# A finer, re-ordered job schedule with paired remainders and eight named PSUM banks in an attention-plus-MLP kernel

## The chip, the cores and the metric

The kernel runs on one core of one Trainium2 chip. The core has TensorE (PE, matmuls; the loading of its weights is shown apart as PEld), VectorE (DVE), ScalarE (ACT), GpSimd (POOL), and SyncE (SP), which here only issues DMAs. Matmul results land in PSUM, which has eight banks of 128 x 512 float32. POOL can't read PSUM, so every bank is emptied by ACT or DVE. The metric is device microseconds for one execution, taken as the median of a few runs; lower is better.

## What is computed

One sequence of 2048 tokens with 512 features. `xn` is the layer norm of `x`. The output is `x` plus attention over `xn` plus an MLP over the layer norm of `xn`:

```python
def _A_ref(x, wq, wk, wv, wo, beta):          # 32 heads of 16, 4 segments of 512 tokens
    for s in range(N):
        qs, ks, vs = q[:, :, s], k[:, :, s], v[:, :, s]
        logits = einsum("bhqd,bhkd->bhqk", qs, ks) * scale + mask
        p = softmax(logits);  a_dot = einsum("bhqk,bhkd->bhqd", p, vs)
        pq = phi(qs);  num = einsum("bhld,bhde->bhle", pq, M);  den = einsum("bhld,bhd->bhl", pq, z) + 1e-6
        o = g * num / den + (1.0 - g) * a_dot
        pk = phi(ks);  M = M + einsum("bhld,bhle->bhde", pk, vs);  z = z + sum(pk)
    return o @ wo
def _B_ref(x, w1, b1, w2, b2):                # 512 -> 1792 -> 512
    return gelu(layernorm(x) @ w1 + b1) @ w2 + b2
xn = layernorm(x)
return x + _A_ref(xn, ...) + _B_ref(xn, ...)
```

The mask is causal within a segment; `phi(t)` is `t + 1` where `t > 0` and `exp(t)` elsewhere.

## The kernel before

**Units.** Attention is cut into 16 units: 4 segments times 4 groups of 8 heads. The MLP is cut into 16 pieces `j`: 8 blocks of 256 tokens times two halves of the 1792 hidden features. Most operands are float32 values split into a high and a low float16, so a product is three matmuls.

**Jobs.** All work is a list of small jobs. `streams()` gives lists of jobs that keep their own order, `ORDER` is one long string in which each letter names a stream, and `plan()` walks the string, takes the next job of the named stream and calls its function. The kernel has a manual schedule: each engine gets its instructions in the order in which the jobs issue them, and waits on semaphores where it needs another's result. So the string is the schedule, for PE and for the queues of ACT, DVE, POOL and SP alike.

The jobs that matter, with their letters as used below:

- `T` (`qk_proj`, matmuls on line 459): projects the queries or keys of a unit, 12 matmuls of 512 columns; ACT and DVE make the high and low halves (477, 481), SP sends them to DRAM, ACT and DVE form `phi` (480, 486 to 492). `Tr` reads them back in a layout in which two heads lie on partitions 0 to 49 and 64 to 113.
- `M` (`m_jobs`, 584 and 591): products of queries with keys, two heads at a time, each in one half of PE's rows and each into its own bank; DVE adds the mask and takes the row maximum. A unit has 12 such jobs: for each of four head pairs one with query block 3 (512 columns), one with blocks 2 and 0 (384 + 128), one with block 1 (256 columns, so half of each bank is used). `R` (`m_row`, 599) turns the maxima into rows, which go over DRAM (`md`) into the query operand (`Rr`).
- `S` (`s_jobs`, 626 and 631): scores transposed, keys on partitions, again two heads in two halves of PE and two banks; ACT takes the exponential into `pt`, POOL zeroes what the causal mask forbids (640). 12 jobs a unit: key block 0 (512 columns), blocks 1 and 3 (384 + 128), block 2 (256).
- `pv`, `PV` (655): the value product, four heads at a time in four column strips of PE; `O` (`o_norm`, 679 to 691): the division and the split of the result; `out` (777): the output projection, added to the token's row `acc` and stored (`st`).
- `K`, `N`, `Z`, `Qd`, `Q`: the memory state `M`, `z` and its use (505 to 568).
- `D` (459 with `w1s`): one hidden tile of the MLP, 12 matmuls of 256 columns; `G` (723): gelu over a piece, with a table load on each side (723 and 839); `H` (730 to 732): split of the activation in POOL, ACT, POOL; `e`, `E` (759): second product, three matmuls of 512 columns, summed over seven jobs in one bank, then added to `acc` by DVE (763).
- `X`, `Y`, `Xt`, `Yt`: layer norm and transposes (385 to 448). `wl`, `wm`, `wf`, `ws`: load of the weights, sums of squares (299), scale (332 to 350), split into two float16 (362 to 367). `hold` (273): a memset of one column that makes the weight loads behind it wait.

**PSUM.** Seven banks are a rotating pool `dense`, and the eighth, `eacc`, is kept for the sum of the MLP's second product.

**SP.** One queue holds nearly all DMAs in the order of the jobs; only the bias rows (740) go out on POOL's queue.

Of the kernel before, what the change touches and what calls it, by code (L numbers as in the profile page):

```python
# [19 lines left out]
P = 128  # L20
D = 512
# [33 lines left out]
NAMES = "abcdefghijklmnopqrstuvwxyzABCDEFGHIJKLMNOPQRSTUVWXYZ"  # L55


def streams():
    keys, queries, nat, qk_back, maxi, m_back, soft, vals_p, heads, memo, vals, norm, again, hid, act, mlp, outs, accs, wts = (
        [] for _ in range(19))  # L60
    for i in range(NU):
        s, g = divmod(i, NG)
        keys.append(("T", i, 1))
        queries.append(("T", i, 0))
        qk_back += [("Tr", i, 1), ("Tr", i, 0)]
        m_back.append(("Rr", i))
        maxi += [("M", i, n) for n in range(12)] + [("R", i)]
        for h, ts in enumerate(((0, 2), (1, 3))):
            soft += [("S", i, t, n) for t in ts for n in range(3)]
            vals_p += [("pv", i, h, kb) for kb in range(3)] + [("PV", i, h)]  # L70
        heads += [("O", i, k) for k in range(3)]
        if s:
            memo += [("Z", i), ("Qd", i), ("Q", i)]
        if s < NSEG - 1:
            nat.append(("N", i))
            memo.append(("K", i))
        if g == 0:
            vals += [("V", s, b) for b in range(4)]
            outs += [("out", s, b) for b in range(4)]
    norm += [("X", 0, 0, 0), ("X", 0, 1, 0), ("X", 0, 0, 1), ("X", 0, 0, 2), ("X", 0, 1, 2)]  # L80
    for n in range(NSEG):
        for b in range(2):
            norm += [("X", n, b, k) for k in range(3)] * (n > 0) + [("Xt", n, b, k) for k in range(2)]
    for n in range(2 * NSEG):
        again += [("Y", n, 0, 0), ("Y", n, 0, 2), ("Yt", n, 0, 0), ("Yt", n, 0, 1)]
    for j in range(NU):
        hf, fh = divmod(j, 2)
        hid += [("D", j, f) for f in range(FH)]
        act += [("G", j)] + [("H", j, c) for c in range(4)]
        for a in range(2):  # L90
            if fh == 0:
                accs += [("A", 2 * hf + a, k) for k in range(2)]
            mlp += [("e", j, a, f) for f in range(FH - 1)] + [("E", hf, a, fh)]
    for m in PARTS:
        wts += [("wl", m, k) for k in range(LOADS[m])]
        if m == "qk":
            wts.append(("hold",))
        if m == "v":
            wts.append(("par",))
    split = [[("wm", m, k) for k in range(SQUARES[m])] + [("wf", m)] + [("ws", m, c) for c in range(len(SPLIT[m]))] +  # L100
             [("gate",)] * (m == "v") for m in PARTS]
    zero = [("zero", 0), ("const",), ("zero", 1)]
    return [norm, again, wts, [("par2",)], zero, keys, queries, nat, qk_back, maxi, m_back, soft, vals_p, heads, memo, vals,
            hid, act, mlp, outs, accs, [("st", n) for n in range(4 * NSEG)]] + split
# [3 lines left out]
    "aacawweeacccccwccaccwawxxxaaxbxxaceyyxxxxdfcbzzzcycxxAizbyyxzgbzyiczAzhzqqAzqqyzqBABjjjAucqgAqjujrpjrjBAcjBAjf"  # L108
    "srpsjjsjAsrbAipsujByikCrcCpssoBjsCsBCjBlBqBssljlquljqljBlsqjjDmBmmmjqhjblsjllsqlljqojlCbrCmmcmmjbakCfCqCqriqnq"
    "rginllhqsallsnugllqojjjmmDmCCmqsCljslljlrrujjjjflssljsarjjmiumimmsDsrssjasrnhsrskDnqasssjlqnjllsaaqlllsqqjjmmm"  # L110
    "umarjqjlslsjlaqljsasljsbljsDjjDbfsmmmmrbjssrnokbDgDssqrqinollqqllilqqljsnsjrjjmmmmqjrlsjlsshljlsjlsqjlsjjjmmmm"
    "rofpjinropnkgnipllsltvulltvlujjprjjjmmmmosjljsjltvblujjslblotvjjlsmrmmmsjhnskrnssfsqloqsilulqlollsgqinqqmmmmbo"
    "llossjlsljusljshsljbjmmmuramrjqunjqrnfqjqrsijjsoqnjjsrsssoqjskgsqqslallsssaslilsolrrjqjjjummjmmharjssjlqjarssl"
    "jlasjljrsljqsjlaqksmsmammnoqnssaqslsalblsbofnllioolbgbmmmmbhiqllqqllqjlqjlqjromrmmmjnjrnfppjjsjopjjjspsjorsojn"
    "rksbightvslllitvllsqljsosjjjmmmmjtvljsuusuljlusslljtljjsvrmrmmmnjjqrnqqqjkfssroqrsiqllsnollsgillsquosbmmmmbssl"
    "osjllsjslsjlsljhrujarjmmmmjnjqrnqfuisqsjssrjjorjqqssonjksgssoasslllsssllqqilrajjqrjjqqjarmmmmjjsarljssrssjljsl"
    "salllaqjsasusmmmmnqjqnqhjskassoanbsofllblolillgbimmmmobollflqljlqljqjjrmmmmrnjjrqqpnbjjjsrspsjjosspjoqnjkigtvr"
    "sslllpoliltvljssbjjjmmmmqjlsljssljlssljtvjrjtvjrlmmjqusjmrmnsrnkfqssllsqouqurqqulolliluusgoqsnmmmmibsllsbsslls"
    "sjljqjlursjmmmmqrnjrjnfjqqrssjisjjoqssrjjqoqsjsrkgssisrsnqrqllolssqsqljrlsjrjsssjlsjmmjjmmqljqljslljljjqlsjkru"
    "mmmmssnrnsslllssslllnossmmmmrllllsllorsrmmmmnsssssnnssssstvtvtvtv"  # L120
# [3 lines left out]
def plan():  # L124

    todo = [iter(st) for st in streams()]
    tab = "E"
    for c in "".join(ORDER):
        key = next(todo[NAMES.index(c)])
        k = key[0]  # L130
        need = "G" if k == "G" else "E" if k in ("S", "Qd") or k == "O" and key[2] == 0 or k == "T" and (
            key[1] >= NG if key[2] == 0 else key[1] < NU - NG) else tab
        yield key, None if need == tab else need
        tab = need
# [3 lines left out]
def infini_mixer_kernel(ctx: ExitStack, tc: tile.TileContext, x, wq, wk, wv, wo, beta, w1, b1, w2, b2, out):  # L138
# [216 lines left out]
    def w_split(m, n):  # L355
# [5 lines left out]
        if SPLIT[m][n] == "V":  # L361
            A.activation(h, r, AF.Copy, scale=s)
            V.scalar_tensor_tensor(l, r, s, h, op0=OP.mult, op1=OP.subtract)
        else:
            G.tensor_scalar(r, r, s, 0.0, op0=OP.mult, op1=OP.add)
            A.activation(h, r, AF.Copy)
# [39 lines left out]
    def norm_apply(tok, tiles, twice, act):  # L406
        for j, t in enumerate(tiles):
# [8 lines left out]
    def ln(kind, n, b, part):  # L416
# [11 lines left out]
        else:  # L428
            norm_apply(tok, lt[kind, n, b], kind == "Y", (kind, n, b) == ("X", 0, 1))
# [38 lines left out]

    def qk_proj(i, which):
        s, g = divmod(i, NG)  # L470
        w, rows, d = ((wqs, (0, 32, 16), qd[i % 2]), (wks, (0, 16, 32), kd[i % 2]))[which]
# [5 lines left out]
        A.activation(hl[:, 0, :], p, AF.Copy, scale=float(2 ** -16))  # L477
        if phi:
            e = sb.tile([P, 512], F32, name=("phq", "phk")[which])
            A.activation(e, p, AF.Exp, scale=qkcol(2, 1 - which, g))  # L480
        V.scalar_tensor_tensor(hl[:, 1, :], p, float(2 ** -16), hl[:, 0, :], op0=OP.mult, op1=OP.subtract)  # L481
# [3 lines left out]
        if phi:  # L485
            V.tensor_scalar(e, e, 1.0, qkcol(3, 1 - which, g), op0=OP.min, op1=OP.mult)
            if which == 0:
                V.scalar_tensor_tensor(e, p, 0.0, e, op0=OP.max, op1=OP.add)
            else:
                if s:  # L490
# [378 lines left out]
```

## Time and profile before

| what | value |
|---|---|
| median of 3 runs | 762.66 us (762.06 to 762.82) |
| span of the profiled execution | 761.0 us |
| TensorE busy | 723.0 us, 95% of the span, 5189 matmul records |
| VectorE busy | 547.7 us, 72% |
| ScalarE busy | 528.8 us, 69% |
| GpSimd busy | 353.7 us, 46% |
| mean granted TensorE clock | 0.989 of full speed |

The span runs from the first to the last instruction of one profiled execution; the median of the runs stands 1.66 us above it. Durations below come from this execution. Times in a row of the timeline are the start and then the length, both in us; matmuls overlap, so the distance from one start to the next tells more than the length. A float32 matmul has two records on PE in some cases, so 5189 records are 4595 matmuls of the program. A granted clock below 1 means that PE ran a part of the stretch at half speed. "Idle before" and "<-" tell how long an engine stood still ahead of a row and what it had waited for.

### The profile page before, as it was taken

To read this page: it belongs to the slowest core of one execution; us is meant where nothing else is said; L and a number is where in the kernel's file an instruction comes from. 1 tells how busy PE (TensorE), PEld (TensorE's weight loads), DVE (VectorE), ACT (ScalarE), POOL (GpSimd) and SP (SyncE) were. 2 spreads that over 40 slices of the span, in tenths; PEclk is the share of its full clock that TensorE was granted. 3 is DMA by queue.
4 is the path that set the end of the run, shared out by engine and by line. 5 is a ranking of instruction groups with operands and counts; after the bars stand their busy time and mean duration, and the time that the engine had idled before them with its cause. 6 is when DMAs were issued, how large, how long until landed. Compare 5 with 4: busy or idle time off the path is not lost.

```text
span 761.0 us, 14513 instructions
## 1 busy us (share of the span) xinstructions
PE 723.0 (95%) x5189; PEld 378.0 (50%) x5189; DVE 547.7 (72%) x1677; ACT 528.8 (69%) x908; POOL 353.7 (46%) x544
## 2 busy tenths in 40 slices
PE   2689999999999999999999999999999999999987
PEld 1364565455644455554454455455555445455433
DVE  5599878898685857888567674979759574777622
ACT  5887898778785568485783577758585577856970
POOL 4465646654524443453434163536335235345461
PEclk9899999999999999999999999999999999999989
DMA  6975213411203224120311324131240314211001
GB/s 184 328 202 157 74 47 103 92 43 52 63 22 112 78 71 100 44 69 19 102 39 39 101 66 118 36 79 30 52 124 1 93 43 104 64 45 43 17 1 56
DMA packets 54085, 59.16 MB, mean 78 GB/s; under 512 B 5039, under 2 KB 40893, under 8 KB 54013
## 3 DMA queue, kind: packets, MB, share of 16 engines
q1 hardware_dynamic: 51708, 54.04, 24.8%
q0 software_dynamic: 2304, 4.20, 3.4%
q8 instruction: 41, 0.67, 0.4%
q14 instruction: 32, 0.25, 0.1%
HBM read 41.18 MB, written 17.04 MB: 77 GB/s over the span
## 4 chain that ended last, share of the span: by engine, by line
PE 83%; ACT 7%; DVE 5%; issue 2%; DMA 1%; POOL 1%; SPq 1%; DVEq 0%; ACTq 0%; POOLq 0%
PE dense L459 33%; PE eacc L759 18%; PE dense L655 9%; PE dense L777 6%; PE dense L626 5%; PE dense L584 5%; ACT pt L631 2%; PE dense L532 2%; PE dense L540 1%; PE dense L560 1%; PE dense L444 1%; DMA mhl<-in_B_b_dram 1%; DVE dense L591 1%; ACT hT L723 1%; DMA nN<-in_A_x_dram 1%
## 5 line engine op out<-in xcount | busy, mean ns | idle before, releaser
L591 DVE CUSTOM_DVE_ANT_0 dense<-dense,mask 128x512 f32<-128x512 f32 (+3 forms) x512 | 241.3, 516 | 21.5 <-PE dense L584 14.0
L631 ACT ACTIVATE pt<-dense,qkcs 128x512 f32<-128x512 f32 (+1 forms) x384 | 205.5, 627 | 31.5 <-PE dense L626 31.2
L759 PE MATMUL eacc<-w2s,hT 128*128 128x512 f16 x672 | 171.6, 382 | 2.0 <-DVE acc L763 1.0
L640 POOL TENSOR_SCALAR_AFFINE_SELECT pt<-pt 128x256 f32<-128x256 f32 x256 | 101.0, 424 | 141.9 <-ACT pt L631 141.2
L459 PE MATMUL dense<-yT,w1s 128*128 128x256 f16 x1344 | 161.4, 273 | 2.9 <-DVE yT L448 2.1
L459 PEld LDWEIGHTS <-w1s 128*128 128x128 f16 x1344 | 127.8, 98 | 36.9 <-issue 15.2
L732 POOL TENSOR_TENSOR hT<-hh,hT 128x512 f16<-128x512 f32 x64 | 69.2, 1081 | 88.2 <-ACT hT L731 88.2
L759 PEld LDWEIGHTS <-hT 128*128 128x128 f16 x672 | 58.6, 98 | 78.2 <-issue 26.4
L655 PE MATMUL dense<-pt,vt 128*32 128x512 f32 (+3 forms) x1024 | 79.0, 440 | 0.1
L591 DVE DVE_READ_ACCUMULATOR2_ANT mc<- 128x1 f32 x512 | 72.6, 142 | 0.0
L731 ACT ACTIVATE hT<-hh 128x512 f16<-128x512 f32 x64 | 36.6, 572 | 42.8 <-POOL hh L730 42.7
L584 PE MATMUL dense<-kst,qst 48*128 48x512 f16 (+3 forms) x512 | 62.8, 300 | 1.8 <-ACT pt L631 0.9
L626 PE MATMUL dense<-qst,kst 50*128 50x512 f16 (+3 forms) x512 | 61.2, 301 | 2.5 <-ACT pt L631 1.4
L730 POOL TENSOR_SCALAR hh<-hT,sc 128x512 f32<-128x512 f32 x64 | 42.6, 666 | 40.6 <-ACT hT L723 38.4
L481 DVE SCALAR_TENSOR_TENSOR hl<-dense,hl 128x512 f16<-128x512 f32 x32 | 22.0, 688 | 54.7 <-ACT phq L480 40.1
L655 PEld LDWEIGHTS dense<-pt,vt 128*32 128x32 f32 x1024 | 32.6, 110 | 45.7 <-issue 32.3
L716 ACT ACTIVATE hT<-dense,b1t,sc 128x256 f32<-128x256 f32 x64 | 36.0, 564 | 18.9 <-PE dense L459 18.3
L459 PE MATMUL dense<-xnT,wks 128*128 128x512 f16 x192 | 48.2, 405 | 0.0
L459 PE MATMUL dense<-xnT,wqs 128*128 128x512 f16 x192 | 45.8, 390 | 0.1
L459 PE MATMUL dense<-wvs,xnT 128*128 128x512 f16 x192 | 43.9, 379 | 0.1
L777 PE MATMUL dense<-wos,oT 128*128 128x512 f16 x192 | 43.7, 380 | 0.0
L626 PEld LDWEIGHTS <-kst 50*128 50x128 f16 x512 | 21.2, 94 | 43.5 <-issue 36.8
(223 smaller groups left out, 951.5 us busy)
## 6 DMA issues: line engine op xcount, KB each, us to landing
xt<-in_A_x_dram SPq DMA_DIRECT2D x30, 256.0 KB
kd<-hl SPq DMA_DIRECT2D x48, 128.0 KB
kst<-kd SPq DMA_DIRECT2D x32, 192.0 KB
qd<-hl SPq DMA_DIRECT2D x48, 128.0 KB
qst<-qd SPq DMA_DIRECT2D x32, 192.0 KB
acc<-in_A_x_dram SPq DMA_DIRECT2D x16, 256.0 KB
acc<-in_B_b_dram POOLq DMA_DIRECT2D x16, 256.0 KB, 4.3
out_dram<-acc SPq DMA_DIRECT2D x16, 256.0 KB
```

Source lines behind the costliest of these rows:

```text
L459: T.matmul(p, wsl(ws, k, a), xsl(xs, k, b), start=s0 and i == 0, stop=s1 and i == 3 * n - 1)
L584: T.matmul(p[:, o:o + n], stk[i, 0][r, t, P * qb:P * qb + P], stk[i, 1][r, t, :n], start=True, stop=True)
L591: V.tensor_tensor_reduce(p[:, o:o + n], p[:, o:o + n], mask[:, 512 - n:], 1.0, -3e38, OP.add, OP.max, mc[i][:, 4 * b + t, qb:qb + 1])
L626: T.matmul(p[:, o:o + n], stk[i, 1][r, t, P * kb:P * kb + P], stk[i, 0][r, t, P * kb:], start=True, stop=True)
L631: A.activation(e[:, OFF[kbs[0]]:OFF[kbs[0]] + o], p[:, :o], AF.Exp, scale=qkcs[:, 1, i % NG:i % NG + 1])
L640: G.affine_select(v, v, pattern=[[0, 2], [1, P]], compare_op=OP.is_ge, fill=0.0, base=0, channel_multiplier=-1)
L655: T.matmul(p[32 * c:32 * c + 32, P * kb:], vt[s, kb][:, 4 * g + c, 16 * odd:16 * odd + 32], pt[i, 2 * c + odd][:, OFF[kb]:OFF[kb] + LEN[kb ...
L730: G.tensor_scalar(t, hz[:, z, :], col(SHH + j % 2), 0.0, op0=OP.mult, op1=OP.add)
L731: A.activation(hT[:, z, 0, :], t, AF.Copy)
L732: G.tensor_tensor(hT[:, z, 1, :], t, hT[:, z, 0, :], op=OP.subtract)
L759: T.matmul(p, t[:, u, P * a:P * a + P], w2s[:, fo, v, :], start=fi == 0 and n == 0, stop=fi == FH - 1 and n == 2)
L777: T.matmul(p, o[:, u, P * b:P * b + P], wos[:, g, v, :], start=i == 0, stop=i == 3 * NG - 1)
```

## The change

- **Finer jobs.** Several jobs are cut in two to six, each with its own stream, so that the string can place the parts apart: `T` into projection, low half with its DMAs (`Tv`) and `phi` (`Tw`); `S` into scores and the causal selects (`Sg`); `O` into six steps; `H` and `ws` into three; `Qd` into three; the two tiles of a layer norm into one each. The instructions are the same.
- **Paired remainders.** The 256-column remainders of two head pairs share one pair of banks: 10 jobs of `M` and 10 of `S` a unit instead of 12 and 12.
- **One ring of eight named banks.** `eacc` goes; each bank is a tile with a name of its own, and a second string, `BANKS`, says which one the next user takes.
- **A new `ORDER`** of all jobs, 1731 instead of 1385, with new letters. Among much else, `hold` stands earlier, the first weight pieces are loaded ahead of the third and fourth tile of `x`, and the transposed bias comes behind the first projection.

```diff
 ORDER = (
-    "aacawweeacccccwccaccwawxxxaaxbxxaceyyxxxxdfcbzzzcycxxAizbyyxzgbzyiczAzhzqqAzqqyzqBABjjjAucqgAqjujrpjrjBAcjBAjf"
...
+    "gaeaeaeRgeeRgTaRTeTTaaaTSebTbebbXTUecUSUeheciXjfUedZZZX3lcZm00d10kY0N2Y12Yk0cN301yl2III03V1eI42oVoWeOIeI4mU5YI"
...
+BANKS = (
+    "01234567012345670132450371247503126475032147501326750132675043520674352076453207465032734265073542076134520671"
...
-    dps = ctx.enter_context(tc.tile_pool(name="dps", bufs=7, space=PSUM))
-    eps = ctx.enter_context(tc.tile_pool(name="eps", bufs=1, space=PSUM))
+    dps = ctx.enter_context(tc.tile_pool(name="dps", bufs=1, space=PSUM))
...
+    banks = iter("".join(BANKS))
+
     def dense():
-        return dps.tile([P, 512], F32, name="dense")
+        return dps.tile([P, 512], F32, name="dense" + next(banks), bufs=1)
...
+    MJOBS = [[(t, 3)] if k == 0 else [(t, 2), (t, 0)] for t in range(4) for k in range(2)]
+    MJOBS = MJOBS[:4] + [[(0, 1), (1, 1)]] + MJOBS[4:] + [[(2, 1), (3, 1)]]
+
+    def m_job(i, j):
...
+        for t, qb in MJOBS[j]:
+            n = P * (qb + 1)
+            for b, p in enumerate(ps):
+                r = slice(64 * b, 64 * b + KM)
+                T.matmul(p[:, o:o + n], stk[i, 0][r, t, P * qb:P * qb + P], stk[i, 1][r, t, :n],
+                         start=True, stop=True)
+            o += n
...
+    SJOBS = [[(t, kb) for kb in kbs] for h in range(2) for t in (h, h + 2) for kbs in ((0,), (1, 3))]
+    SJOBS = SJOBS[:4] + [[(0, 2), (2, 2)]] + SJOBS[4:] + [[(1, 2), (3, 2)]]
+
+    def s_job(i, j):
...
+        for b, p in enumerate(ps):
+            for k in range(2 if job[0][1] == 2 else 1):
+                t, kb = job[k]
+                c, n = (256 * k, 256) if kb == 2 else (0, o)
+                A.activation(pt[i, 4 * b + t][:, OFF[kb]:OFF[kb] + n], p[:, c:c + n], AF.Exp,
+                             scale=qkcs[:, 1, i % NG:i % NG + 1])
+
+    def s_mask(i, j):
...
+                G.affine_select(v, v, pattern=[[0, 2], [1, P]], compare_op=OP.is_ge, fill=0.0,
+                                base=0, channel_multiplier=-1)
...
                     if f0 == 0:
-                        pe = eps.tile([P, 512], F32, name="eacc")
-                        hold.append(pe)
+                        hold.append(dense())
```

More of the change, by code (lines that the diff above doesn't have):

```diff
@@ L77, in streams @@
         if g == 0:
[L78 to L85, printed above, removed]
+            put("val", *[("V", s, b) for b in range(4)])
@@ L94, in streams @@
+    put("store", *[("st", n) for n in range(4 * NSEG)])
     for m in PARTS:
-        wts += [("wl", m, k) for k in range(LOADS[m])]
-        if m == "qk":
-            wts.append(("hold",))
-        if m == "v":
[L99 to L104, printed above, removed]
@@ L467, in infini_mixer_kernel @@
     zs = {}
+    prj = {}
     def qk_proj(i, which):
         s, g = divmod(i, NG)
[L471 removed]
+        w = (wqs, wks)[which]
         p = dense()
```

309 lines of the change are left out of this document (180 added, 129 removed).

## The prediction

> **What bounds the kernel now.** I read the page first: busy time, the slices, the chain.
>
> ```profile
> span 761.0 us, 14513 instructions
> PE 723.0 (95%) x5189; PEld 378.0 (50%) x5189; DVE 547.7 (72%) x1677; ACT 528.8 (69%) x908; POOL 353.7 (46%) x544
> PE   2689999999999999999999999999999999999987
> PEclk9899999999999999999999999999999999999989
> PE 83%; ACT 7%; DVE 5%; issue 2%; DMA 1%; POOL 1%; SPq 1%; DVEq 0%; ACTq 0%; POOLq 0%
> ```
>
> TensorE is the bound: 723 of 761 us busy, nine tenths or more in 35 of 40 slices, 83% of the chain. No matmul is taken away, so a gain must come from time in which PE stands still or is "busy" without streaming columns. Second view, the busy time by stretch (columns: stretch, its length, PE, PEld, DVE, ACT, POOL, granted clock, DMA share, GB/s):
>
> ```profile
> 0.00:19.00 19.00, 4.23 (x18) 3.74 (x18) 10.94 (x38) 10.04 (x21) 8.84 (x22) 1.00 0.64 184
> 19.00:38.00 19.00, 11.43 (x34) 5.87 (x35) 11.12 (x49) 15.48 (x28) 8.38 (x9) 0.82 1.07 328
> 38.00:57.00 19.00, 16.83 (x131) 11.84 (x130) 18.54 (x46) 16.66 (x28) 13.21 (x12) 1.00 0.72 203
> 57.00:114.00 57.00, 56.45 (x427) 31.75 (x425) 48.77 (x169) 48.35 (x86) 32.09 (x46) 1.00 0.34 93
> 114.00:171.00 57.00, 56.26 (x428) 29.07 (x427) 49.57 (x170) 44.15 (x80) 34.99 (x53) 0.97 0.33 80
> 722.00:761.00 39.00, 32.73 (x174) 12.98 (x172) 10.51 (x15) 15.82 (x30) 16.66 (x27) 0.91 0.07 28
> ```
>
> Of the 38 us in which PE is idle, 24.5 lie in the first 57 us (57 less 4.23, 11.43 and 16.83) and 6.3 in the last 39. Between them PE looks full. The timeline shows that it isn't: look at when the next row starts.
>
> ```profile
> 416.97 2.75 PE L777 MATMUL dense<-wos,oT 128*128 128x512 f16 x12
> 419.56 0.81 PE L759 MATMUL eacc<-w2s,hT 128*128 128x512 f16 x3
> ...
> 420.95 2.76 PE L777 MATMUL dense<-wos,oT 128*128 128x512 f16 x12
> 423.65 0.61 PE L626 MATMUL dense<-qst,kst 50*128 50x512 f16 x6
> ...
> 424.85 1.47 PE L459 MATMUL dense<-yT,w1s 128*128 128x256 f16 x12
> 426.25 0.28 PE L626 MATMUL dense<-qst,kst 50*128 50x256 f16 x2
> 426.37 0.38 PE L584 MATMUL dense<-kst,qst 48*128 48x512 f16 x2
> 426.69 1.47 PE L759 MATMUL eacc<-w2s,hT 128*128 128x512 f16 x6
> ```
>
> Twelve matmuls of 512 columns take 2.59 us (416.97 to 419.56) if another full-array matmul follows, 2.70 (420.95 to 423.65) if a score follows, whose 50-row operands use half of the array each. Back it costs the same: the pair of maxima at 426.37 takes 0.32 us for 512 columns, where the score pair before it took 0.12 for 256 (0.24 for 512, so 0.08 to 0.10 more). From score to maxima, half to half, nothing is lost. So each change between full array, halves, and the four column strips of the value product costs about 0.10 us, though PE counts as busy.
>
> **The change part by part.**
>
> *Order: fewer changes of the array's shape.* In the order of the built programs' matmuls I counted the places where the shape changes: 434 before, 309 after. Runs of scores and maxima between full-array work fall from 183 to 128, and are then two or three jobs in 118 of 128 cases. 125 changes × 0.10 = 12.5 us, all on PE's own line, where nothing hides it. Ends: 125 × 0.08 = 10, and 13.
>
> ```profile
> L459 PEld LDWEIGHTS <-w1s 128*128 128x128 f16 x1344 | 127.8, 98 | 36.9 <-issue 15.2
> ```
>
> The lost time is that of one weight load, 98 ns. The Trainium skill ("TensorE: Matmul & The Clock Gate", Part 3, The mechanism and what overlaps) says that weight loads overlap running matmuls only when the row groups differ. By that sentence alone every load in a full-array stream would be exposed too, a change of shape would cost nothing extra, and this term would be 0, the sum 12.5 us smaller. The trace disagrees: twelve loads hide in 2.59 us.
>
> *Remainders paired.* Two 256-column remainders share a pair of banks: a unit takes 10 jobs of maxima and 10 of scores instead of 12 and 12. The instructions stay: 512 reductions, 384 exponentials (a score remainder still has two of 256 columns per bank), 256 selects, the same matmuls. Only bank turns fall, 768 to 640. By itself 0; its worth is in the runs above and the banks below.
>
> *Eight named banks, accumulator in the ring.* No instruction. In the built order I summed PE's work between the last matmul into a bank and the first of the bank's next use: median 3.2 us before, 4.0 after; lowest 1% 0.5 before, 0.8 after. So more time for the engine that empties it.
>
> *Finer jobs.* Same instructions, in smaller groups, so that a select or second half no longer sits right behind its exponential on POOL's, ACT's or DVE's queue. ACT has 884 rows in both programs. On the idle sides this costs nothing; it is what the order uses.
>
> *Start.*
>
> ```profile
> 2.21 0.43 SPq L424 DMA_DIRECT2D nD<-in_A_x_dram  x1
> 7.93 0.63 ACT L299 ACTIVATE wks<-wks 128x512 bf16<-128x512 f32 x1 [5.83 <-DMA wks<-in_A_wk_dram]
> 10.63 0.06 DVE L273 MEMSET wks<- 128x1 f32 x1
> 10.71 0.37 SPq L240 DMA_DIRECT2D wks<-in_A_wk_dram  x1
> 22.52 0.28 PE L794 MATMUL dense<-ident,mhl 14*128 14x14 f32 x1 [2.00 <-DMA mhl<-in_B_b_dram]
> 22.73 5.22 PE L459 MATMUL dense<-xnT,wks 128*128 128x512 f16 x12
> 32.71 0.59 PE L332 MATMUL dense<-am,ones 128*128 128x2 f32 x2 [4.65 <-ACT w1s L299]
> 42.27 2.67 PE L459 MATMUL dense<-yT,w1s 128*128 128x256 f16 x23 [1.87 <-DVE yT L448]
> ```
>
> Before, the one-column memset that the second weight load waits for stands on DVE behind the first layer norm: it runs at 10.63, and SP issues that load at 10.71. In the new order it is DVE's first instruction, and the load comes right behind the six first loads, at about 3.5 us: up to 7 us sooner, with all that follows on SP's queue (w1, and the next tiles of x). Against it, tiles nN and nD now stand behind the first pieces of wk and wq: two issues of some 0.5 us, so the first norm is about 1 us later. The transposed bias, which held the first projection for 2.00 us, moves behind it; six ACT instructions (some 0.63 us each) move behind the second half of yT; one more projection (2.59 us at full clock) runs before the first hidden job. ACT is idle for 14.8 of the first 57 us (57 less 10.04, 15.48 and 16.66), 7.93 less a table load of them ahead of its first operand, so it can give 7 to 8 at most. Best case 7.0 + 2.6 = 9.6 gained, worst 0 (ACT's own work holds everything). I take 6, since ACT was at 15.48 and 16.66 of 19 us.
>
> *After the start.* The ACT work put off comes due in 57 to 171 us, where ACT stood at 48.35 and DVE at 48.77 of 57. I counted the ACT work that is ahead of PE's tenth to hundred-fortieth us of work: 123 us before, 126 after. PE covers that stretch in some 5 us less (some 24 changes of shape fewer, and the run below). I take 2 us of new waits; ends 0 and 6.
>
> *The run of eight.* Before, the order had one run of eight jobs of scores and maxima:
>
> ```profile
> 131.59 4.43 ACT L631 ACTIVATE pt<-dense,qkcs 128x512 f32<-128x512 f32 x8
> ...
> 134.18 1.10 PE L584 MATMUL dense<-kst,qst 48*128 48x256 f16 x4 [0.21 <-ACT pt L631]
> ...
> 136.27 4.45 PE L459 MATMUL dense<-xnT,wks 128*128 128x512 f16 x12
> ```
>
> PE crawled behind ACT from about 133 to 136, and the next twelve matmuls took 4.45 us (from start to start 4.38) instead of 2.59, in the stretch whose granted clock is 0.97. The new order has no run over four. I take 3 us, ends 0 and 4.
>
> *The round trip of the row maxima.*
>
> ```profile
> 711.50 0.27 PE L599 MATMUL dense<-ident,mc 128*32 128x128 f32 x1
> 712.43 0.30 SPq L604 DMA_DIRECT2D md<-mhl  x1
> 713.84 0.53 SPq L609 DMA_DIRECT2D qst<-md  x2
> ```
>
> From the transposition at 711.50 to the read's issue it is 2.3 us, with the landing perhaps 4.5. PE's work between that transposition and the unit's first score job is 4.8 to 10.9 us before, 3.5 to 9.9 after; three units fall under 5. So PE may wait in those: 0 to 3 us in all, I take 0, since only one is under the 4.5. The other trip, from projection to maxima, grows (least 7.6 before, 8.9 after).
>
> *Tail.*
>
> ```profile
> 718.48 6.18 ACT L631 ACTIVATE pt<-dense,qkcs 128x512 f32<-128x512 f32 x12
> 729.38 6.20 ACT L631 ACTIVATE pt<-dense,qkcs 128x512 f32<-128x512 f32 x12
> 735.87 3.24 PE L655 MATMUL dense<-pt,vt 128*32 128x512 f32 x32
> ```
>
> The last unit's exponentials are 12.4 us of ACT, with 8.8 us of PE work (counted likewise) between its first and last score job. After it is 14.0, with fewer maxima left over. PE was idle for 6.3 us there. I take 3.5, ends 0 and 6.
>
> *Sum*: 12.5 + 6 − 2 + 3 + 3.5 = 23 us, from 761.0 to 738. The median of the runs stands 1.7 above the span (762.66), so 740 (739.7).
>
> **The rivals.**
>
> (1) *The early gains are given back.* ACT and DVE hold the first 171 us, so start and run of eight bring nothing, waits of 6 us appear, the tail stays: 12.5 − 6 = 6.5, time 756; with part of it some 752. For it: 86% of DVE and 85% of ACT in 57 to 114. Against it: an order that keeps the backlog from standing before PE, ACT idle for 8.6 us in that stretch.
>
> (2) *Slower: the runs outpace the emptying.*
>
> ```profile
> L631 ACT ACTIVATE pt<-dense,qkcs 128x512 f32<-128x512 f32 x256 | 157.8, 695 | 24.6 <-PE dense L626 24.4
> PE dense L626 <- ACT pt L631: 1.4, 4, 0.7
> ```
>
> A run of three fills six of eight banks in about 0.8 us of PE; emptying takes up to six times 0.62 us (157.8 / 256) on ACT, 3.7 us, or as much on DVE, whose passes have about that length. Two banks are left, one often held by the accumulator. If the full-array work after a run needs a bank too soon, PE stands. 72 runs have three jobs or more: at 0.32 us each the whole gain is gone, at 0.5 us it is 36 − 23 = 13 slower, 776. Against it: before, scores waited for ACT's emptying in 4 places, 1.4 us in all, and the distances above grew. The Trainium skill's "TensorEngine Tiling (Array Packing)", PSUM Bottleneck, warns of this: a faster tiled array can make the copies out of PSUM the limit. Here each engine is at most 86% busy by stretch, so it doesn't hold on average.
>
> (3) *More than that*: all ends at once, 13 + 9.6 + 4 + 6 = 32.6, and no new wait: 730.
>
> **How the numbers follow.** Forecast 0.64 (its own range 732 to 748), rival (1) 0.17, rival (2) 0.09, rival (3) 0.10. The range 730 to 756 takes in the first, (1) and most of (3). About 0.2% (1.5 us) is what a measurement tells from no change; only a mixture of (1) and (2) falls there: faster 0.89, same 0.02, slower 0.09.
>
> **What would show it.** Right: twelve full-array matmuls still 2.59 and 2.70, but 309 changes; PE's dense hidden jobs from about 36 us instead of 42.27; a clock of 1.00 in 114 to 171; last output projection ending earlier behind the last value product. Wrong: PE rows with idle time "<-ACT pt" or "<-DVE mc" in many places, a clock under 1.00 in the middle, PE rows of weight loads that wait for banks, or no earlier start because the first norm waits for nN and nD.

## The result and the profile after

The changed kernel takes 735.37 us (median, 733.36 to 735.74), beside 762.74 for the kernel before on the same chip: a ratio of 0.9635, 95% interval 0.9617 to 0.9652. The forecast was 740, with 730 to 756 as its range. The profiled execution spans 733.4 us, 27.6 less than before.

The page of the changed kernel, its span, TensorE's busy time, slices and granted clock, and the shares of the chain:

```profile
span 733.4 us, 14559 instructions
PE 698.3 (95%) x5189; PEld 379.9 (52%) x5189; DVE 534.2 (73%) x1677; ACT 520.9 (71%) x908; POOL 352.9 (48%) x544
PE   2899999999999999999999999999998999999897
PEclk9999999999999999999999999999999999999999
PE 63%; DVE 22%; DMA 5%; issue 4%; ACT 4%; POOL 1%; SPq 1%; POOLq 0%; DVEq 0%; ACTq 0%
```

TensorE is busy for 95% as before, with as many matmul records. Its idle time is 35.1 us (733.4 less 698.3), where it was 38.0. So 24.7 of the 27.6 us were counted as busy before: they were changes of shape, half clock and waits too short to be shown. The chain now runs through VectorE for 22%, where it was 5%; 15 of the 22 are VectorE's passes over the maxima (line 653 there, 12% and 3% in the page's chain by line). The busy time by stretch, changed kernel, columns as in the prediction:

```profile
0.00:19.00 19.00, 5.37 (x21) 4.37 (x22) 10.40 (x38) 11.60 (x25) 8.81 (x22) 1.00 0.94 273
19.00:38.00 19.00, 16.33 (x75) 8.14 (x75) 15.05 (x56) 16.13 (x28) 7.76 (x8) 0.91 0.76 234
38.00:57.00 19.00, 16.73 (x121) 10.13 (x120) 18.45 (x54) 17.49 (x27) 14.30 (x17) 1.00 0.99 276
57.00:114.00 57.00, 56.07 (x448) 33.53 (x447) 50.21 (x166) 49.73 (x93) 34.57 (x47) 1.00 0.32 82
114.00:171.00 57.00, 55.55 (x447) 30.49 (x446) 52.67 (x188) 48.42 (x85) 37.99 (x56) 1.00 0.32 76
695.00:734.00 39.00, 34.39 (x209) 14.43 (x208) 12.12 (x17) 17.28 (x34) 19.63 (x30) 0.98 0.11 35
```

Of the 57 us of the start TensorE is busy for 38.4 instead of 32.5. The clock stands at 1.00 in 114 to 171 (0.97 before) and 0.98 at the end (0.91).

To see where the 27.6 us come from, I took all matmuls of each trace, gave each its columns' time (2.59 us for twelve of 512, so 0.216 for 512 columns; half of that for matmuls that run two at a time, a quarter for four; float32 records at about twice that), and 0.098 us to each change of the array's shape. The columns come to 648.2 us in both kernels. So the first row of the table is a count times a price, not a measured time; whether the price is right is tested below. What is left of the span (idle, half clock, short waits):

| | before | after | difference | forecast |
|---|---|---|---|---|
| changes of shape, 434 and 309 | 42.5 | 30.3 | −12.2 | −12.5 |
| rest in 0 to 57 us | 34.2 | 28.1 | −6.1 | −6 |
| rest in 57 to 171 | 7.5 | 5.1 | −2.4 | −1 (+2 − 3) |
| rest in 171 to 627 | 12.3 | 11.0 | −1.3 | 0 |
| rest from 627 to the end | 16.2 | 10.7 | −5.5 | −3.5 |

The stretches are of equal time, not of equal work; the start and the end can be compared row by row. Timeline of the changed kernel:

```profile
3.84 0.43 SPq L284 DMA_DIRECT2D wks<-in_A_wk_dram  x1
...
35.53 4.30 PE L505 MATMUL dense<-yT,w1s 128*128 128x256 f16 x35 [0.85 <-DVE yT L494]
...
686.55 0.28 PE L659 MATMUL dense<-ident,mc 128*32 128x128 f32 x1 [0.94 <-DVE mc L653]
...
691.52 0.92 PE L688 MATMUL dense<-qst,kst 50*128 50x512 f16 x6 [0.99 <-DMA qst<-md]
...
698.94 2.36 PE L722 MATMUL dense<-pt,vt 128*32 128x512 f32 x32
...
709.21 2.42 PE L722 MATMUL dense<-pt,vt 128*32 128x512 f32 x32
711.56 7.30 PE L831 MATMUL dense<-w2s,hT 128*128 128x512 f16 x33
718.69 10.80 PE L849 MATMUL dense<-wos,oT 128*128 128x512 f16 x48
```

The second load of wk is issued at 3.84 instead of 10.71, the dense hidden jobs start at 35.53 instead of 42.27. In the tail the two value products take 2.36 and 2.42 us. Before they took 3.59 and 3.24, and this stretch of the kernel before, which the prediction didn't price, says why the second was slow (the first row is busy time by stretch, the others are timeline; the first value product, at 724.01, ran at full clock):

```profile
732.00:736.00 4.00, 4.00 (x13) 1.09 (x13) 0.75 (x1) 3.58 (x8) 2.50 (x7) 0.50 0.00 0
```

```profile
724.01 3.59 PE L655 MATMUL dense<-pt,vt 128*32 128x512 f32 x32
...
729.02 0.37 PE L626 MATMUL dense<-qst,kst 50*128 50x512 f16 x1 [0.76 <-ACT nD L664]
730.12 0.37 PE L626 MATMUL dense<-qst,kst 50*128 50x512 f16 x1 [0.72 <-ACT pt L631]
...
732.58 2.08 PE L540 MATMUL dense<-phq,mst 128*128 128x512 f32 x2
734.45 1.49 PE L759 MATMUL eacc<-w2s,hT 128*128 128x512 f16 x3
```

In 732 to 736 the granted clock was 0.50: two float32 matmuls took 2.08 us that take 1.02 in the changed kernel, three MLP matmuls 1.49 instead of 0.82, the value product at 735.87 3.24 instead of 2.36. That is 2.6 us which the new tail, without TensorE's waits at 728 to 732, doesn't lose.

There are new waits too. Waits of TensorE, first the kernel before, then the changed one (us in total, times, longest):

```profile
PE dense L599 <- DVE mc L591: 0.3, 1, 0.3
```

```profile
PE dense L659 <- DVE mc L653: 4.2, 7, 1.6
```

The transposition of a unit's row maxima now comes so close behind the last maxima that TensorE waits 4.2 us for VectorE, in seven units (1.3 us of it in 57 to 171, 2.0 in 171 to 627, 0.9 in the last unit). It is the largest of TensorE's waits for the passes over the maxima.

### The profile page after: what moved, and what is told of

It is laid out like the page before. It is cut to its first block, busy times and chain, and to the rows that moved or that the text cites. A ratio compares the mean times of both kernels' runs of the same rounds, so it can differ in the third digit from the quotient of the medians.

```text
span 733.4 us, 14559 instructions
## 1 busy us (share of the span) xinstructions
PE 698.3 (95%) x5189; PEld 379.9 (52%) x5189; DVE 534.2 (73%) x1677; ACT 520.9 (71%) x908; POOL 352.9 (48%) x544
## 4 chain that ended last, share of the span: by engine, by line
PE 63%; DVE 22%; DMA 5%; issue 4%; ACT 4%; POOL 1%; SPq 1%; POOLq 0%; DVEq 0%; ACTq 0%
PE dense L505 23%; PE dense L831 15%; DVE dense L653 12%; PE dense L722 7%; PE dense L849 5%; PE dense L688 4%; PE dense L646 3%; DVE mc L653 3%; PE dense L621 1%; PE dense L589 1%; PE dense L601 1%; DMA qd<-hl 1%; PE dense L490 1%; DMA qst<-qd 1%; DMA pt<-in_A_wq_dram 1%
## 5 line engine op out<-in xcount | busy, mean ns | idle before, releaser
L653 DVE CUSTOM_DVE_ANT_0 dense<-dense,mask 128x384 f32<-128x384 f32 (+3 forms) x512 | 243.1, 513 | 32.3 <-PE dense L646 24.9
L831 PE MATMUL dense<-w2s,hT 128*128 128x512 f16 x672 | 167.2, 380 | 0.5 <-DVE mc L653 0.3
L709 POOL TENSOR_SCALAR_AFFINE_SELECT pt<-pt 128x256 f32<-128x256 f32 x256 | 103.1, 438 | 98.7 <-ACT pt L695 98.0
L505 PEld LDWEIGHTS <-w1s 128*128 128x128 f16 x1344 | 129.6, 98 | 36.8 <-issue 12.5
L831 PEld LDWEIGHTS <-hT 128*128 128x128 f16 x672 | 60.8, 98 | 71.5 <-issue 18.2
L722 PE MATMUL dense<-pt,vt 128*32 128x512 f32 (+3 forms) x1024 | 75.8, 436 | 0.0
L801 POOL TENSOR_SCALAR hh<-hT,sc 128x512 f32<-128x512 f32 x64 | 42.5, 664 | 57.7 <-ACT hT L791 54.0
L753 POOL TENSOR_TENSOR nN<-nN,oT 128x512 f32<-128x512 f32 x16 | 20.5, 1279 | 80.8 <-DVE oT L574 80.8
L646 PE MATMUL dense<-kst,qst 48*128 48x384 f16 (+3 forms) x512 | 54.8, 299 | 4.3 <-DVE mc L653 2.1
L688 PE MATMUL dense<-qst,kst 50*128 50x384 f16 (+3 forms) x512 | 52.5, 298 | 1.7 <-DMA qst<-md 1.0
L505 PE MATMUL dense<-xnT,wks 128*128 128x512 f16 x192 | 46.0, 390 | 1.4 <-ACT xnT L493 0.8
L786 DVE TENSOR_SCALAR hT<-dense,sc,b1t 128x256 f32<-128x256 f32 x48 | 25.7, 539 | 24.5 <-PE dense L505 24.3
```

Source lines behind the costliest of these rows:

```text
L505: T.matmul(p, wsl(ws, k, a), xsl(xs, k, b), start=s0 and i == 0, stop=s1 and i == 3 * n - 1)
L646: T.matmul(p[:, o:o + n], stk[i, 0][r, t, P * qb:P * qb + P], stk[i, 1][r, t, :n], start=True, stop=True)
L653: V.tensor_tensor_reduce(p[:, o:o + n], p[:, o:o + n], mask[:, 512 - n:], 1.0, -3e38, OP.add, OP.max, mc[i][:, 4 * b + t, qb:qb + 1])
L688: T.matmul(p[:, o:o + n], stk[i, 1][r, t, P * kb:P * kb + P], stk[i, 0][r, t, P * kb:], start=True, stop=True)
L709: G.affine_select(v, v, pattern=[[0, 2], [1, P]], compare_op=OP.is_ge, fill=0.0, base=0, channel_multiplier=-1)
L722: T.matmul(p[32 * c:32 * c + 32, P * kb:], vt[s, kb][:, 4 * g + c, 16 * odd:16 * odd + 32], pt[i, 2 * c + odd][:, OFF[kb]:OFF[kb] + LEN[kb ...
```

## The experiments

The forecast was near. What had to be tested were its single terms, above all those put at zero: bank numbers, pairing, ring. A wait for a bank is counted below like this: for each tile the end of its last reader on ACT or DVE was taken from the trace, and the start of the first matmul of the tile that gets its bank next; where TensorE stood for over 0.12 us ahead of that matmul, and it started within 0.25 us of the reader's end, the gap is a wait for the bank. Before: 13 of them, 4.6 us. Changed kernel: 20, 7.1 us.

**Other bank numbers.** The order is untouched; the bank string gives each tile the bank whose last reader stands earliest in the list of jobs.

```diff
-    "01234567012345670132450371247503126475032147501326750132675043520674...
+    "01234567012345670132457013245071362450713645071362507136250473625047...
```

> The changed kernel with its order kept, and its string of bank numbers replaced by another: each tile takes the bank whose last reader stands earliest in the list of jobs. 810 of 985 numbers differ. My theory (banks are not what decides; distances between a bank's uses are several us in both): no change, 735.4, within 1.5 us. Rival (the bank numbers were chosen to fit the emptying, and carry part of the gain): 738 to 745, with waits of score and maxima matmuls for 'ACT pt' and 'DVE mc' adding up to more.

Measured: 748.38 us (744.19 to 750.10), ratio 0.9810 [0.9783, 0.9838]: 13 us slower than the changed kernel, with no instruction and no place in the order altered. My theory fell. Waits for a bank come to 17.2 us in 35 places, and in 29 of them (15.8 us) another bank stood empty. The longest in the middle, on the timeline:

```profile
126.18 0.32 PE L688 MATMUL dense<-qst,kst 50*128 50x384 f16 x1 [0.16 <-DVE mc L653]
127.99 0.38 PE L688 MATMUL dense<-qst,kst 50*128 50x384 f16 x3 [1.49 <-DVE mc L653]
```

The second score of the pair is given the bank of a maxima job whose reduction VectorE finishes only at 127.9, behind a projection's low half and a weight split in its queue; two other banks had been emptied by ACT at 124.5 and 125.1. Over the whole run the waits for banks are 10.1 us longer than in the changed kernel, whose profiled execution was 14.5 us shorter; that they are the cause is tested next.

**Banks by the time of emptying.** So the question was whether it is the queue behind the reader that matters. Here each tile gets the bank whose last reader ended earliest in the trace of the changed kernel.

```diff
-    "01234567012345670132450371247503126475032147501326750132675043520674...
+    "01234567012354761032541360254163027541263054102634710236471053160475...
```

> The changed kernel with its order kept, and each tile given the bank whose last reader ended earliest in the trace of the changed kernel (not earliest in the list of jobs, as in the first run of this study). 776 of 985 tiles then follow the same tile into their bank as in the changed kernel; in the first run it was 494. Theory (the 13 us of the first run are waits for banks whose reader stands in a long queue, while another bank is empty): 733 to 737, and waits for a bank of some 4 to 8 us as in the changed kernel, not 16. Rival (the numbers matter for something else, or any departure from the string costs): 740 to 748.

Measured: 735.48 us (734.22 to 736.66), 0.9646 [0.9625, 0.9666]: the whole 13 us are back. Waits for a bank fall to 5.0 us in 14 places, in none of them is another bank empty. That is 12.2 us of waits less than in the first experiment. So a string that names banks by when they will be empty is worth 13 us against one that goes by their place in the list, and the waits carry most of it.

**More changes of shape.** In 30 and in 60 runs of scores and maxima the last job goes behind the full-array job that follows it (banks by the rule of the first experiment, which is the comparison here):

```diff
  S(3,4)  M(4,0)
- M(4,1)  e(3,0,3)
+ e(3,0,3)  M(4,1)
  e(3,0,4)
```

(one of the 30; only jobs with matmuls are shown.)

> The changed kernel, in which the last job of 30 runs of scores and maxima is moved behind the full-array job that follows: 60 changes of the array's shape more (369 for 309), the matmuls the same, banks given as in the run with other bank numbers. Theory (0.10 us per change, on TensorE's own line): 60 x 0.098 = 5.9 us more, 741.3. Rival (a change of shape is paid by waits that are there anyway, or shorter runs ease the emptying): 735 or less.

> The same in 60 runs: 120 changes more, 429 for 309, nearly the 434 of the kernel before. Theory: 120 x 0.098 = 11.8 us more, 747.1, on one line with the run of 60. Rival (emptying): 735 or less, or no line.

Measured: 753.74 (751.72 to 757.38) and 754.73 (753.10 to 757.20), against 748.38: +5.4 for 60 changes, +6.4 for 120, where 5.9 and 11.8 were expected. The first dose fits, the second pays half. At the same time the waits for banks fall from 17.2 to 13.2 and 10.3 us: shorter runs leave more time for the emptying. Adding that back, 120 changes cost 6.4 + 6.9 = 13.3 us, 0.11 each, and 60 changes 9.4, 0.16 each. This is rough: the times are medians, whose spread here is some 3 us, and the waits come from single profiled executions (the one with 60 changes was the slowest of its six). A least-squares fit of TensorE's busy time over the fourteen profiles of this case, by the number of changes and by the time lost to the clock, gives 0.10 us a change, standard error 0.015.

The traces also show the price change by change. In the kernel before, 121 runs of scores and maxima stand behind and ahead of full-array matmuls with no idle time and at full clock. The way in and the way out together take 0.206 us beyond the columns (median; half of the runs lie within 0.204 to 0.208). In the changed kernel it is 0.208 (60 runs), in the run with 120 more changes 0.205 (120 runs). So the price holds, at 0.103 a change. The rival was right in part too: in a kernel short of empty banks half of it is given back.

Where the time goes is seen on the weight loads, in a stretch of the kernel before that the prediction showed:

```profile
419.35 0.53 PEld L759 LDWEIGHTS <-hT 128*128 128x128 f16 x3
...
423.65 0.33 PEld L626 LDWEIGHTS <-kst 50*128 50x128 f16 x6 [0.42 <-issue]
```

From full array to full array the load starts 0.21 us ahead of its matmul (419.56), under the matmul before. Ahead of a score the loading stands still for 0.42 us, and the load starts with its matmul (423.65). Over the trace: behind a full-array matmul of 512 columns another's load starts 2 ns after that matmul's start, and the matmul follows at 216 ns (medians of 1260 cases); a score's or maximum's load starts at 308 ns and its matmul at 312 (102 cases). So across a change of shape no weights are loaded ahead. What the load waits for, the 92 ns behind the last column, isn't shown.

**Remainders not paired.** Same order, each 256-column remainder in a pair of banks of its own, taken at the same place (banks by the list, as in the first experiment).

```diff
+        if qb_pair(MJOBS[j]):
+            m_part(i, MJOBS[j][:1])
+            m_part(i, MJOBS[j][1:])
+        else:
+            m_part(i, MJOBS[j])
...
+        for part in ([job[:1], job[1:]] if qb_pair(job) else [job]):
+            s_part(i, part)
```

> The changed kernel with the order kept, and each 256-column remainder in a pair of banks of its own, both pairs taken at the same place of the order: 768 bank turns for 640, no other instruction. Theory (pairing by itself is worth nothing): 735.4 to 737. Rival (banks are short, and the pairing is what makes runs of three possible): 740 or more, with more waits of score and maxima matmuls for the emptying.

Measured: 802.06 us, 1.0520 [1.0483, 1.0558]: 54 us slower than with paired remainders and the same rule for banks, and slower than the kernel before. Waits of TensorE in this run (L658 maxima, L704 scores; mc is emptying by VectorE, pt by ScalarE):

```profile
PE dense L658 <- DVE mc L665: 10.2, 17, 2.0
PE dense L704 <- DVE mc L665: 8.2, 14, 0.9
...
PE dense L704 <- ACT pt L711: 3.2, 5, 1.1
PE dense L658 <- ACT pt L711: 3.0, 5, 1.1
```

Waits for a bank are 53.1 us in 87 places. In 36 of these another bank was empty (20.8 us), so the choice was bad; in 51 (32.3 us) none was: there no other number would have helped. Against the first experiment the waits for banks are 35.9 us longer, and the profiled execution's mean clock of 0.985 for 0.995 goes with some 8 us more. The 54 us hold for two pairs of banks taken at one place; the remainders spread out, as in the order before, weren't tried in the new one.

**Seven banks and the accumulator apart.** Same order, the eighth bank kept for the MLP's sum, as before the change; the other seven by the list.

```diff
-    "01234567012345670132450371247503126475032147501326750132675043520674...
+    "01234560123456012435612435162435012634051376041532604715326041523064...
```

> The changed kernel with the order kept, and the eighth bank used by the MLP's accumulator alone, the other seven by all other tiles, as before the change. Theory (ring of eight worth nothing by itself, since emptying is fast enough): 735.4 to 737. Rival (the runs of three need the eighth bank): 740 or more.

Measured: 780.54 us, 1.0237 [1.0219, 1.0254]: 32 us slower than the ring of eight under the same rule. Waits and one row of the timeline:

```profile
PE dense L831 <- DVE acc L835: 18.5, 13, 3.7
```

```profile
748.63 1.44 PE L831 MATMUL dense<-w2s,hT 128*128 128x512 f16 x3 [3.73 <-DVE acc L835]
```

18.5 us are the MLP's next sum waiting for the one bank it may use, while VectorE still adds the last sum to `acc`. Before the change that was one wait of 1.0 us: the order before kept two sums further apart. The other 25.5 us of bank waits (44.0 in all) come from one bank fewer to choose from and, in part, from the choice: in 30 of these 46 waits (14.7 us) another of the seven was empty. Seven banks numbered by a trace weren't tried.

**The memset late.** In the changed kernel the one-column memset goes back behind the first layer norm.

```diff
  X(0,1) load
- hold
  X(0,0) statistics
+ hold
  wl(QK)
```

> The changed kernel with one instruction moved back: the one-column memset that the second load of wk waits for stands behind the first layer norm on VectorE again. Theory (the memset's place carries the start's gain of 6): the load is issued at about 12, all loads behind it follow, and the time is 740 to 743, up to 8 us later. Rival (other parts of the start carry it: the bias moved, ACT work put off, one projection more): 735 to 737.

Measured: 741.86 us (741.28 to 742.19), 0.9727 [0.9713, 0.9742]: +6.5. Timeline:

```profile
11.98 0.38 SPq L284 DMA_DIRECT2D wks<-in_A_wk_dram  x1
...
15.04 0.63 ACT L343 ACTIVATE wks<-wks 128x512 bf16<-128x512 f32 x1 [7.32 <-DMA wks<-in_A_wk_dram]
...
20.07 1.11 PE L490 MATMUL dense<-ident,nN 128*128 128x128 f32 x4 [5.22 <-ACT nN L456]
...
41.84 4.30 PE L505 MATMUL dense<-yT,w1s 128*128 128x256 f16 x35 [0.85 <-DVE yT L494]
```

The load is 8.1 us later, the hidden jobs 6.3 (41.84 for 35.53), the end as much. In the new order four squares of the later pieces stand on ScalarE ahead of the third tile's normalization (`nN`). ScalarE now waits 7.32 us for the load, and TensorE 5.22 for `nN`. So the new order leans on the early load.

**The memset alone.** The same instruction moved ahead in the kernel before.

```diff
+ hold
  X(0,0) statistics
  wm(qk) wm(qk) zero const X(0,0) apply
- hold
  wl(QK)
```

> The kernel before, with the one-column memset on VectorE ahead of the first layer norm, nothing else moved. Theory (its place alone brings the start's gain): the second load of wk at 3 to 4 us instead of 10.71, and 756 to 758 for 762.7. Rival (ACT's own work or the next loads hold the start): 761 to 763.

Measured: 760.35 us (759.12 to 761.92), 0.9972 [0.9961, 0.9983]: −2.6, where 4.7 to 6.7 were expected. Timeline:

```profile
3.71 0.51 SPq L240 DMA_DIRECT2D wks<-in_A_wk_dram  x1
...
29.73 0.58 PE L332 MATMUL dense<-am,ones 128*128 128x2 f32 x2 [6.18 <-ACT w1s L299]
...
39.28 2.67 PE L459 MATMUL dense<-yT,w1s 128*128 128x256 f16 x23 [1.32 <-DVE yT L448]
```

The load comes 7.0 us sooner, but TensorE now stands 6.18 us for ScalarE's squares of `w1` (4.65 before), and the hidden jobs start 3.0 earlier, not 6.7. The memset is needed for the start's gain (in the new order all is lost without it), but alone it brings less than half. The wait for the squares of `w1` points to ScalarE's order for the rest; that order alone wasn't tried.

**x first.** In the changed kernel the second pair of x tiles is loaded ahead of the first pieces of wk and wq.

```diff
  X(0,0) load
- wl(qk)
  X(0,1) load
+ wl(qk)
  hold
```

> The changed kernel, with the loads of x for the first and the second pair of tiles issued ahead of the first pieces of wk and wq. Theory (the first norm waits to 7.96 for the second pair, and started 1 us earlier before the change): the first transposition some 1 us earlier, 734 to 735. Rival (weights are what the start waits for): 735.4 to 737, the first projection not earlier or later.

Measured: 736.80 us (735.40 to 739.17), 0.9665 [0.9643, 0.9687]: no gain; the median is 1.4 above the changed kernel's, and the two 95% intervals overlap. The profile:

```profile
11.72 1.97 PE L490 MATMUL dense<-ident,xt 128*128 128x128 f32 x8 [1.49 <-POOL xt L458]
...
18.42 0.38 PE L505 MATMUL dense<-xnT,wks 128*128 128x512 f16 x1 [1.06 <-ACT xnT L493]
```

The first transposition is 1.4 us sooner (11.72 for 13.17), but the first projection stands at 18.42, where it was 18.24: ScalarE normalizes the third tile at 13.10, behind the same four squares as before (12.93 there), and the hidden jobs start at 35.47 for 35.53. ScalarE's work on the weights sets the time, as the rival said.

**The tail.** The nine MLP steps that stand between the score jobs of the last unit go ahead of its first score job.

```diff
+ e(14,0,2) ... e(14,1,3)
  S(15,0) S(15,1)
- e(14,0,2) ... e(14,0,6)
  S(15,2) S(15,3) S(15,4)
- e(14,1,0) ... e(14,1,3)
  pv(15,0) ...
```

> The changed kernel, with the nine steps of the MLP's second layer (nine times 0.65 us) that stand between the score jobs of the last unit moved ahead of its first score job, as in the kernel before. Theory (TensorE then waits for ACT's 12.4 us of exponentials, and the clock drops to half as it did before at 732 to 736): 4 us of waits and 2 us of half clock more, 1 us less at the round trip of the row maxima, so 739 to 742. Rival (the tail's gain comes from elsewhere): 734.4, the round trip's 1 us less.

Measured: 739.83 us (738.68 to 742.20), 0.9705 [0.9685, 0.9726]: +4.5. Timeline:

```profile
697.51 0.98 PE L688 MATMUL dense<-qst,kst 50*128 50x512 f16 x9
698.74 0.37 PE L688 MATMUL dense<-qst,kst 50*128 50x384 f16 x3 [0.24 <-ACT pt L695]
699.32 0.27 PE L688 MATMUL dense<-qst,kst 50*128 50x256 f16 x1 [0.20 <-ACT pt L695]
700.47 0.38 PE L688 MATMUL dense<-qst,kst 50*128 50x256 f16 x3 [0.89 <-ACT pt L695]
...
701.83 4.08 PE L722 MATMUL dense<-pt,vt 128*32 128x512 f32 x32
```

Scores wait for ACT's emptying again, the value product takes 4.08 us for 2.36 (its operands come from the same exponentials; at 724.01 the kernel before shows the like, 3.59 at full clock), and the wait for the round trip (0.99 at 691.52) is gone. From the last transposition of maxima to the output projection it is 35.76 us here and 32.14 in the changed kernel, 3.6 more. The size is near what was expected, but partly by luck: the half clock, 2 us of the forecast, didn't come (the granted clock is 1.00 from 695 to 721), and the value products cost more than was thought. The waits here are of 0.20 to 0.89 us, those of the kernel before were of 0.76 and 0.72; why the clock fell there and not here isn't shown.

**Two attempts in the kernel before.** First, 20 full-array jobs moved behind the next run, so that two runs become one (394 changes for 434).

```diff
  S M
- e(...)
  M S
+ e(...)
```

> The kernel before, with 20 full-array jobs moved behind the next run of scores and maxima, so that two short runs become one of three or four: 394 changes of shape for 434, nothing else. Theory (0.10 us per change): 40 x 0.098 = 3.9 us less, 758.8 for 762.7. Rival (longer runs outpace the emptying): 762 or more, with waits for 'ACT pt' and 'DVE mc'.

Measured: 768.33 us (767.72 to 768.79), 1.0075 [1.0061, 1.0088]: 5.4 slower, not 3.9 faster. TensorE's waits in this run:

```profile
PE dense L584 <- DVE phk L492: 2.0, 2, 1.3
PE dense L584 <- ACT pt L631: 1.8, 7, 0.5
PE dense L584 <- DMA qst<-qd: 1.8, 4, 0.6
```

TensorE is idle for 45.9 us instead of 38.0: maxima moved up against emptying (0.9 of the second row was there before) and against the load of their operands, and waits for banks went from 4.6 to 8.9 us. Fewer changes, got by these 20 moves with seven banks in turn and the remainders unpaired, cost more than they save.

Second, the run of eight broken up by a projection and two MLP steps that stood behind it.

```diff
- S(1,1,1) S(1,1,2) M(2,4) S(1,3,0) H H A M(2,5) M(2,6) M(2,7) M(2,8) T(3) S(1,3,1) e e S(1,3,2) M(2,9)
+ S(1,1,1) S(1,1,2) M(2,4) S(1,3,0) H H A T(3) M(2,5) M(2,6) M(2,7) e M(2,8) S(1,3,1) S(1,3,2) e M(2,9)
```

> The kernel before, with its run of eight score and maxima jobs broken up by a projection and two MLP steps that stood behind it (436 changes of shape for 434). Theory (run of eight makes TensorE wait and the clock drop): 759 to 760.5 for 762.7, the granted clock 1.00 in 114 to 171. Rival (those waits come back in the next jobs): 762 to 763.

Measured: 768.09 us (767.28 to 768.41), 1.0072 [1.0059, 1.0084]: 5.1 slower. It tells the theories apart only in part, since my edit made a wait of its own:

```profile
138.48 0.42 ACT L731 ACTIVATE hT<-hh 128x256 f16<-128x256 f32 x1 [1.85 <-POOL hh L730]
138.80 0.58 ACT L477 ACTIVATE hl<-dense 128x512 f16<-128x512 f32 x1
...
139.99 0.69 DVE L481 SCALAR_TENSOR_TENSOR hl<-dense,hl 128x512 f16<-128x512 f32 x1 [4.86 <-ACT phk L480]
...
141.87 0.67 PE L584 MATMUL dense<-kst,qst 48*128 48x256 f16 x2 [3.55 <-DVE phk L492]
```

```profile
138.00:148.00 10.00, 5.56 (x18) 1.28 (x17) 7.48 (x27) 5.63 (x9) 5.00 (x9) 0.75 0.36 82
```

ScalarE's two passes over the projection (477, 480) stand behind an MLP split that waits for POOL. VectorE's second half waits 4.86 us for them, and TensorE 3.55 us until VectorE has made the projection's `phi` (492). The clock is 0.75 in the ten microseconds from 138: it is at half speed from 143.0 to 149.8, which loses up to 3.4 us, where the kernel before loses 1.7 (half speed from 137.0 to 140.4). So the 5.1 us are about the wait and some 1.5 us of clock, and what the run of eight itself cost isn't shown.

## Why the prediction was right, and where it was not

- *Changes of shape* (−12.5): right in mechanism and size. Count as forecast; the price is 0.098 by the prediction's rows, 0.103 by the median over single runs of scores and maxima, 0.10 ± 0.015 by the fit, so −12.2 to −12.9. The sentence of the Trainium skill that was weighed there ("TensorE: Matmul & The Clock Gate", Part 3, The mechanism and what overlaps) would have made this term zero; the loads that start 2 ns after the matmul before them disagree with it, as the runs with 60 and 120 added changes do. "The lost time is that of one weight load" holds for the size only: the load starts 308 ns after the last matmul instead of 2, and its own 98 ns stand behind that.
- *Remainders paired: "by itself 0; its worth is in the runs above and the banks below". Eight banks: "so more time for the engine that empties it".* The direction was right, the size was not seen. With banks by the list the pairing carries 54 us and the eighth bank 32 in this order, and the numbering alone 13. The step that failed is the reading of medians: I summed TensorE's work between two uses of a bank (median 4.0 us) and compared it with the emptying of a few tiles, but the wait hangs on the queue in front of the reader, and on which bank is named. In the changed kernel itself this costs little, so the sum held; put as "no instruction, so nothing" it would have misled anyone who took over the order without the banks.
- *Rival (2), the runs outpace the emptying, 776*: it didn't happen (bank waits 4.6 to 7.1 us), but it is what happens as soon as the ring or the pairing is taken away with banks by the list: 780.5 and 802.1. "TensorEngine Tiling (Array Packing)", PSUM Bottleneck, in the Trainium skill, says that copies out of PSUM may become the limit of a packed array. These two runs agree in part: TensorE waits 44.0 and 53.1 us for banks (18.5 of the 44.0 for the MLP's sum, which isn't packed), but no emptying engine is over 69% busy, and some 15 and 21 us stand where another bank was empty. So it is queues and the choice of banks as much as the rate of the copies. The argument "each engine is at most 86% busy by stretch" left out a row of the prediction's own table: in 38 to 57 us VectorE was busy for 18.54 of 19 us. Its chance of 0.09 was for the kernel as built; the margin was smaller than I thought.
- *Start* (−6): −6.1, and undoing the memset gives 6.5 back. But the cause was told too simply: alone the memset brings 2.6, and in the new order ScalarE's queue depends on it.
- *After the start* (+2 − 3): −2.4 instead of −1. New waits came, 1.3 us instead of 2, but for VectorE at the maxima's transposition and not for the ScalarE work put off. Without them this stretch would be 3.7 us shorter, against the 3 of the run of eight; 1.7 of it is the half clock, which was gone as forecast. What the run of eight cost beside that stays open.
- *Middle* (0): −1.3 at 0.098 a change, −0.8 at 0.103. The waits of over 0.15 us grew there from 4.2 to 6.3 us, 2.0 of them the maxima's transposition (0.3 before), a place that I had not looked at (I priced the trip behind it). So something else got some 3 us shorter, and I can't place it: a part may be the price of a change, whose uncertainty by the fit is 1.5 us for the 103 changes that fell away there (0.015 × 103).
- *Row maxima's round trip* (0 of 0 to 3): 1.0, in the one unit with 3.5 us of work, unit 15.
- *Tail* (−3.5 of 0 to 6): −5.5. Mis-sized: the idle time fell by 2.3 us (6.3 in the last 39 us before, 4.0 from 695 to the end after), less than the 3.5 taken, and the half clock at 732 to 736, some 2.6 us, was left out, though the 0.91 in the quoted row of 722 to 761 showed it.
- *Sum*: −27.6 instead of −23, and a median 2.0 above the span instead of 1.7: 735.4 instead of 740.

## What to carry to other kernels

A schedule with fewer switches of the array's shape is worth its 0.1 us a switch only if the results can go somewhere: order, pairing, ring and bank numbers are one change. Without the pairing or without the ring of eight the new order ended above the kernel before (802.1 and 780.5, both with banks by the list), and plain bank numbers gave back 13 of the 27 us. Where banks are named ahead of time, name them by when the last reader ends in a trace, not by its place in the list; here that was worth 13 us and no instruction. For a forecast, look at single queues in front of a bank's reader, not at busy shares or median distances, and allow for half clock behind TensorE's waits.

## What the runs showed of the hardware

- Between full-array matmuls the next weight load starts with the matmul before it (2 ns behind its start); across a change of the array's shape it starts 308 ns behind it. A change costs 0.10 us, and all of it counts as busy: the two changes around one moved job (0.206 us) cost about as much as a matmul of 512 columns (0.216 us).
- A wait of TensorE can be followed by half clock that costs nearly as much again. After 3.55 us of standing (run of eight broken up) the granted clock was 0.50 from 143.0 to 149.8, up to 3.4 us lost. The length of the wait doesn't tell it alone: in the kernel before, after waits of 0.21 and 0.20 us, it was 0.50 from 137.0 to 140.4, and after waits of 0.76 and 0.72 between few matmuls from 730.9 to 737.7; in the tail experiment, after waits of 0.24, 0.20 and 0.89, it stayed 1.00.
- Half-clock spells differ from one kernel of the same order to the next: mean 0.997 in the changed kernel, 1.000 with measured banks, at the same time (735.37 and 735.48).
